# ScalarE in written order during a band attention, with scores, transposes, values and weight requests moved by a slot

## The chip, the cores and the metric

One core of a Trainium2 chip runs the whole program. The metric is device time in microseconds, and lower is better. Before the change three runs took 681.58, 681.89 and 684.72 us; the median is 681.89 us.

## The reference

Three stages follow each other, all in float32. A causal attention with a sliding window and a few sink keys, for 2 batches, 8 heads, 768 positions and 64 dimensions per head; then a mixer with a low-rank token step (rank 32) and a channel step of 512 to 2048 to 512; then a second mixer with a token step of 768 to 256 to 768 and a channel step of 512 to 1536 to 512.

```python
keep = is_sink | in_window                    # key < n_sink, or 0 <= i - j < window
scores = np.where(keep, scale * q @ k.T, -1e9)
a = softmax(scores); x = a @ v
u = x + (x.T @ U @ V).T;  x = u + relu(u @ w_ch1) @ w_ch2
u = x + (relu(x.T @ w_tok1) @ w_tok2).T;  x = u + relu(u @ w_ch1) @ w_ch2
```

## The kernel before

**Attention in slots.** `band_attention` walks 16 units (2 batches, 4 head pairs, 2 halves of the sequence) of three query blocks of 128 each: 48 slots, numbered from 0. In a slot two heads are worked together, over the 224 keys that a block can see. A slot has these steps, by name and line:

- `band_scores` (L191): four matmuls into two PSUM banks, one bank a head (`sc`).
- `band_soft` (L202, L206): for each head VectorE masks and scales into `sm` and takes the minimum `nb`; then ScalarE makes the exponentials `pr` and their sum `den`.
- `band_turn` (L217): TensorE transposes `pr` into `tp`; `band_keep` (L222) copies that to `pt`, on ScalarE for the first block of a unit and on VectorE for the other two.
- `band_values` (L235): the products with the values, into `ot`. `band_out` (L244) copies, `band_back` (L249) transposes back, `band_scale` (L256, L257) divides by the sums on VectorE.

In the kernel before, slot t writes the scores and the softmax of block t, the transposes of block t-2 and the values of block t-4. `load` requests the input of block t+3 (288 KB, `qk`) in slot t; `band_load_values` requests 480 KB a unit. Five input buffers exist. All requests go through SyncE's queue, which stands in written order.

**Work beside the attention.** Between the steps of a slot `weave` lets two side streams advance, each held to a budget per step. One, `lead_stream`, decodes weights: a piece of 512 columns (512 KB of 64-bit words, tile `raw`) is requested with `fetch` (L394), ScalarE takes its absolute value (`clamp`, L402, tile `c`), GpSimd limits it (L403), VectorE rebuilds the float in three steps (L409, L411, L413), and `split` writes a high part on ScalarE (L120) and a low part on GpSimd (L121). There are 15 such pieces during the attention: one of U, two of V, twelve of weights `w`. Three `raw` buffers exist; the first three pieces are requested together at the start and the next with each piece that is done. `FEEDS` says after how many finished units a matrix may be decoded. The other side stream, the fills, is the first mixer's token step (`mix_down`, `mix_up`) and two narrow passes through four of its 16 pairs of weight tiles (`hidden`, `gather`: tiles `hp`, `hh`, `hl`, `accs`).

**What sets the order.** Each engine runs its instructions strictly one after the other. In the attention TensorE and SyncE follow the written order (`manual_schedule` with `MANUAL | ORDERED`). The instructions of ScalarE, VectorE and GpSimd are placed by a planner with its own estimate of when their inputs are there; it may move them ahead of where they are written.

**After the attention** (`layers`, `late_weights`) the same decode and the same channel passes go on with TensorE in written order, and the pieces that are left run through the same `fetch` with three buffers.

Of the kernel before, what the change touches and what calls it, by code (L numbers as in the profile page):

```python
# [10 lines left out]
I32 = mybir.dt.int32  # L11
# [9 lines left out]
P = 128  # L21
# [18 lines left out]
MANUAL = {mybir.EngineType.SP}  # L40
# [1 line left out]
SPREAD = {0: (0.3, 0.3, 0.3, 0.4), 1: (0.7, 0.6, 0.6, 0.7)}  # L42
CHUNK, HOLD = 4, 3
AHEAD = 3
DMA_LAG = 6
WARM = 3
CAP = 1.5
PACE = (9.0, 0.7, 9.0, 9.0)
# [29 lines left out]
class Net:  # L78
# [184 lines left out]
    def band_attention(self, xs):  # L263
        tc = self.tc
        units = [(b, hp, half) for b in range(B) for hp in range(NP) for half in range(2)]
        n = len(units)
        with tc.tile_pool(name="ald", bufs=2) as ld, tc.tile_pool(name="asb", bufs=2) as sb:
            self.sb = sb
            st = [None] * n

            raws = {}

            def load(t):
                if t < 3 * n:
                    raws[t] = self.band_load(t, ld)

            def scale(u):
                self.band_scale(st[u], xs[units[u][0]])
                self.finished = u + 1
                if u + 1 == SWITCH:  # L280
                    self.phase = 1

            def slots():
                for t in range(3 * n + 7):
                    u, ii = divmod(t, 3)
                    if u < n:
                        if ii == 0:
                            st[u] = {"unit": units[u]}
                            self.band_tiles(st[u], sb)
                        self.band_scores(st[u], ii, raws.pop(t))  # L290
                        for e in range(2):
                            self.band_soft(st[u], ii, e, sb)
                        load(t + AHEAD)
                        if ii == 1:
                            self.band_load_values(st[u], ld)
                    yield t
                    u, ii = divmod(t - 2, 3)
                    if 0 <= u < n:
                        self.band_turn(st[u], ii)
                        self.band_keep(st[u], ii)  # L300
                    yield t
                    u, ii = divmod(t - 4, 3)
                    if ii < 2 and 0 <= u < n:
                        for z in ((0, 1), (2,))[ii]:
                            self.band_values(st[u], z)
                        if ii == 1:
                            self.band_out(st[u])
                    if ii == 2 and 0 <= u < n:
                        self.band_back(st[u])
                        scale(u)  # L310
                    yield t

            with tc.manual_schedule(engines=MANUAL | {mybir.EngineType.DVE}):
                self.limits()
                self.band_masks()
                for t in range(AHEAD):
                    load(t)

            with tc.manual_schedule(engines=MANUAL | ORDERED):
                self.weave(slots(), SPREAD)  # L320


# [67 lines left out]


    def fetch(self, src, p0, n):
        raw = self.wp.tile([P, 2 * PIECE], I32, tag="raw", name="raw", bufs=3)[:, :2 * n]
        self.nc.sync.dma_start(raw, src[:, 2 * p0:2 * (p0 + n)])  # L394
        return raw

# [30 lines left out]
    def lead_stream(self):  # L427
        nc, one = self.nc, self.one
        uh, ul = [one.tile([P, NS * RANK], F32R, name=f"u1{z}") for z in "hl"]
        self.vh, self.vl = [one.tile([P, S], F32R, name=f"v{z}") for z in "hl"]  # L430
        pieces = []
        for k, after in enumerate(FEEDS):
            if k > 1:
                self.lead.append(self.weight_tiles(k - 2))
            hi, lo = ((uh, ul), (self.vh, self.vl))[k] if k < 2 else self.lead[k - 2]
            src = self.ins["UV"[k]] if k < 2 else self.ins["w1"][k - 2]
            total = hi.shape[1]
            for p0 in range(0, total, PIECE):
                n = min(PIECE, total - p0)
                pp = slice(p0, p0 + n)  # L440
                pieces.append((after, src, p0, n, hi[:, pp], lo[:, pp], k if p0 + n == total else None))
        raws = {}

        def fetch(k):
            if k < len(pieces):
                raws[k] = self.fetch(*pieces[k][1:4])

        for k in range(3):
            fetch(k)
        yield 0, 0, 0, 0, DMA_LAG  # L450
        yield 0, 0, 0.6, 0.8
        nxt = self.clamp(raws.pop(0))
        for k, (after, _, _, n, hi, lo, done) in enumerate(pieces):
            word, c = nxt
            yield 0, 0, 0, 0, 1
            yield "after", after
            if k + 1 < len(pieces):
                yield 0, 0, 0.6, 0.8
                nxt = self.clamp(raws.pop(k + 1))
            yield from self.assemble(word, c)  # L460
            yield 0, 0, 0, 0, 1
            yield 0, 0, 0.52, 1.23
            self.split(hi, lo, f32(c), nc.scalar.copy, nc.gpsimd)
            yield 0, 0, 0, 0, 2
            fetch(k + 3)
            if done == 0:
                self.u4 = one.tile([P, NS, 4, RANK], F32R, name="u4")
                for c in range(4):
                    src = (ul if c % 2 else uh).rearrange("p (s r) -> p s r", r=RANK)
                    yield 0, 0, 0, 0.3  # L470
                    nc.gpsimd.tensor_copy(self.u4[:, :, c, :], f32(src))
            elif done:
                self.fed = done
# [324 lines left out]
    def whole(self, xs, attention):  # L798
        tc = self.tc
        self.turns, self.phase, self.finished, self.fed = {}, 0, 0, 0  # L800
        with ExitStack() as ctx:
            self.ps = ctx.enter_context(tc.tile_pool(name="ps", bufs=1, space=PSUM))
            self.one = ctx.enter_context(tc.tile_pool(name="one", bufs=1))
            self.two = ctx.enter_context(tc.tile_pool(name="two", bufs=2))
            self.wp = ctx.enter_context(tc.tile_pool(name="wp", bufs=1))
            os_ = [t.rearrange("p s d -> p (s d)").rearrange("p (a c) -> p a c", a=ND) for t in (xs[1], xs[0])]
            self.right = ctx.enter_context(ExitStack())
            x1 = self.right.enter_context(tc.tile_pool(name="x1", bufs=1, side="right"))
            xs = [xs[0], x1.tile([P, NS, DM], F32, name="x1")]
            us = [self.u_tiles(0), None]  # L810
            self.lead, self.sides, self.low = [], [], {}

            def narrow(c):
                cc = slice(c * NARROW, (c + 1) * NARROW)
                return self.channel_pass(us[0], LEAD, cc, os_[0], 6, 1)

            fills = []
            for what in FILLS.split():
                if what[0] == "c":
                    fills.append(((0, 1), narrow, (int(what[1]),)))  # L820
                else:
                    b, d = int(what[1]), int(what[2])
                    if what[0] == "d":
                        fills.append(((0, 1), self.mix_down, (b, d, xs[b], self.nc.gpsimd)))
                    else:
                        fills.append(((0, 1), self.mix_up, (b, d, xs[b], os_[b], us[b], self.nc.gpsimd)))
            self.add_side([((0, 0), self.lead_stream, ())])
            self.add_side(fills)
            attention(xs)
            self.drain(last=1)  # L830
            left = self.sides.pop()
            self.phase = 2
            self.late = ctx.enter_context(tc.tile_pool(name="late", bufs=1, reuse_waits="tile"))
            self.ahead = {g: self.weight_tiles(g) for g in range(len(self.lead), RING)}
            us[1] = self.u_tiles(1)
            with tc.manual_schedule(engines=ORDERED):
                self.ring = dict(enumerate(self.lead))
                self.uses = {g: B if g < LEAD else 2 * B for g in self.ring}
                self.fed = len(self.lead)
                self.add_side([((0, 0), self.late_weights, ())])  # L840
                self.mixed, self.tok = {}, None
                late = [((0, 0), self.mix_up, (1, d, xs[1], os_[1], us[1], self.nc.vector)) for d in range(ND)]
                late.insert(1, ((0, 0), self.mix_down, (1, ND - 1, xs[1], self.nc.vector)))
                self.add_side(late)
                self.weave(self.rest(left, self.layers(us, os_)), PACE)
# [82 lines left out]
```

## Time and profile before

| | us |
|---|---|
| median of three runs | 681.89 |
| the profiled execution | 679.99 |
| its span, first to last instruction | 678.1 |
| TensorE busy in the span | 642.8 |
| VectorE busy | 374.0 |
| ScalarE busy | 226.4 |
| GpSimd busy | 185.8 |

TensorE is busy 95% of the span and has a mean granted clock of 0.97 of full speed. Busy time is an average over two stages: the attention, which ends near 193 us, and the channel passes behind it. A busy TensorE at half clock gets half the work done, so both its idle time and its clock are to be read, stretch by stretch.

### The profile page before, as it was taken

How to read it: one execution, taken by the hardware profiler on the slowest of the kernel's cores; microseconds unless marked ns; L12 is line 12 of the kernel's file. 1: busy time of each engine (PE TensorE's matmuls, PEld its weight loads, DVE VectorE, ACT ScalarE, POOL GpSimd, SP SyncE). 2: the span in 40 equal slices, each digit the busy share in tenths (PEclk: the TensorE clock that was granted, in tenths of full speed). 3: DMA queues.
4: the chain of work that ended last, by engine and by line, in shares of the span. 5: the costliest groups of instructions: out<-in, count | busy, mean ns of one | idle time of the engine just before them, and what ended most of it. 6: DMA issues, size and time to landing. Idle time of an engine off the chain costs nothing.

```text
span 678.1 us, 11317 instructions
## 1 busy us (share of the span) xinstructions
PE 642.8 (95%) x4454; PEld 602.2 (89%) x4454; DVE 374.0 (55%) x792; ACT 226.4 (33%) x552; POOL 185.8 (27%) x208
## 2 busy tenths in 40 slices
PE   7699888889999999999999999999999999999996
PEld 3467657777899999999999999999999999999996
DVE  5676667747355147988882344786241377422223
ACT  4465555435222123433331133533231233211110
POOL 4342424303011025444440022762040244200000
PEclk8889699899999999999999999999999999999999
DMA  7936566455000003343330010313000032000112
GB/s 235 276 118 194 166 215 191 141 175 188 1 1 1 1 17 131 114 129 133 128 128 32 1 63 1 124 67 121 1 1 0 1 125 94 2 0 1 48 47 98
DMA packets 30047, 59.49 MB, mean 88 GB/s; under 512 B 2720, under 2 KB 15648, under 8 KB 29984
## 3 DMA queue, kind: packets, MB, share of 16 engines
q1 hardware_dynamic: 29984, 58.67, 26.8%
q8 instruction: 37, 0.61, 0.4%
q14 instruction: 26, 0.21, 0.1%
HBM read 55.51 MB, written 3.15 MB: 86 GB/s over the span
## 4 chain that ended last, share of the span: by engine, by line
PE 83%; DMA 6%; DVE 5%; ACT 2%; issue 1%; SPq 1%; POOL 1%; ACTq 0%; DVEq 0%; POOLq 0%
PE hp L126 33%; PE accs L652 33%; DMA raw<-in_w 6%; PE ot L235 3%; PE gp L126 3%; PE sc L191 2%; PE tp L217 2%; PE up L126 2%; PE tp L126 2%; DVE c L413 1%; DVE c L411 1%; PE xtp L559 1%; PE xtp L126 1%; ACT pr L206 1%; PE xp L586 1%
## 5 line engine op out<-in xcount | busy, mean ns | idle before, releaser
L126 PE MATMUL hp<-uh,wh 128*128 128x384 f32 (+1 forms) x464 | 155.6, 335 | 5.8 <-DVE hl L633 5.8
L633 DVE SCALAR_TENSOR_TENSOR hl<-hp,hh 128x384 fp32r<-128x384 f32 (+1 forms) x116 | 62.8, 541 | 177.5 <-ACT hh L632 176.7
L652 PE MATMUL accs<-hh,wh 128*128 128x384 f32 (+1 forms) x464 | 154.1, 335 | 0.0
L126 PE MATMUL hp<-uh,wl 128*128 128x384 f32 (+1 forms) x464 | 153.5, 331 | 0.0
L126 PE MATMUL hp<-ul,wh 128*128 128x384 f32 (+1 forms) x464 | 153.4, 331 | 0.0
L652 PE MATMUL accs<-hh,wl 128*128 128x384 f32 (+1 forms) x464 | 152.0, 330 | 0.0
L632 ACT ACTIVATE hh<-hp 128x384 fp32r<-128x384 f32 (+1 forms) x116 | 55.7, 480 | 260.7 <-PE hp L126 260.5
L121 POOL TENSOR_TENSOR wl<-c,wh 128x512 fp32r<-128x512 f32 x56 | 76.2, 1363 | 182.5 <-ACT wh L120 180.3
L652 PE MATMUL accs<-hl,wh 128*128 128x384 f32 (+1 forms) x464 | 97.0, 329 | 0.0
L126 PEld LDWEIGHTS hp<-uh,wh 128*128 128x128 f32 x464 | 87.7, 189 | 9.2 <-DVE hl L633 6.9
L652 PEld LDWEIGHTS accs<-hh,wh 128*128 128x128 f32 x464 | 87.7, 189 | 2.5 <-issue 2.0
L126 PEld LDWEIGHTS hp<-ul,wh 128*128 128x128 f32 x464 | 87.8, 189 | 0.0
L126 PEld LDWEIGHTS hp<-uh,wl 128*128 128x128 f32 x464 | 87.7, 189 | 0.0
L652 PEld LDWEIGHTS accs<-hh,wl 128*128 128x128 f32 x464 | 87.7, 189 | 0.0
L652 PEld LDWEIGHTS accs<-hl,wh 128*128 128x128 f32 x464 | 80.3, 188 | 0.0
L403 POOL TENSOR_SCALAR c<-c 128x512 f32<-128x512 f32 (+2 forms) x65 | 46.1, 709 | 99.2 <-ACT c L402 96.9
L660 DVE TENSOR_TENSOR x<-accs,x 128x384 f32<-128x384 f32 (+1 forms) x118 | 58.7, 556 | 15.1 <-PE accs L652 15.0
L402 ACT ACTIVATE c<-raw 128x512 f32<-128x512 f32 (+2 forms) x65 | 43.0, 662 | 52.8 <-DMA raw<-in_w 27.1
L411 DVE SCALAR_TENSOR_TENSOR c<-raw,c 128x512 int32<-128x512 int32 (+2 forms) x65 | 57.4, 883 | 1.9
L206 ACT ACTIVATE pr<-sm,nb 128x224 f32<-128x224 f32 x96 | 45.4, 474 | 26.9 <-DVE nb L202 26.9
L413 DVE SCALAR_TENSOR_TENSOR c<-raw,c 128x512 int32<-128x512 int32 (+2 forms) x65 | 53.6, 824 | 1.4
L409 DVE TENSOR_SCALAR c<-c 128x512 int32<-128x512 int32 (+2 forms) x65 | 42.3, 651 | 16.9 <-POOL c L403 16.8
(144 smaller groups left out, 713.5 us busy)
## 6 DMA issues: line engine op xcount, KB each, us to landing
raw<-in_w SPq DMA_DIRECT2D x56, 512.0 KB, 3.7
qk<-in_qk SPq DMA_DIRECT2D x47, 288.0 KB, 4.1
vy<-in_vy SPq DMA_DIRECT2D x16, 288.0 KB, 4.3
vx<-in_vx SPq DMA_DIRECT2D x16, 192.0 KB, 3.5
raw<-in_t SPq DMA_DIRECT2D x6, 512.0 KB, 3.5
out<-x SPq DMA_DIRECT2D x16, 192.0 KB, 2.0
raw<-in_V SPq DMA_DIRECT2D x1, 512.0 KB, 5.6
x<-in_qk SPq DMA_DIRECT2D x1, 288.0 KB, 3.3
```

The costliest lines, as they stand in the source:

```text
L121: sub.tensor_tensor(lo, src, f32(hi), ALU.subtract)
L126: self.nc.tensor.matmul(out, lhsT=w, rhs=x, start=start and i == 0, stop=stop and i == n - 1, **kw)
L206: nc.scalar.activation(st["pr", ii][:, e], sm, AF.Exp, bias=nb[:, ii, e:e + 1], scale=-1.0, accum_out=den[:, ii, e:e + 1],)
L402: nc.scalar.activation(f32(c), f32(word[:, :, 1]), AF.Abs)
L403: nc.gpsimd.tensor_scalar(f32(c), f32(c), LARGE, SMALL, ALU.min, ALU.max)
L409: nc.vector.tensor_scalar(c, c, 5, 2, ALU.logical_shift_left, ALU.logical_shift_right)
L411: nc.vector.scalar_tensor_tensor(c, word[:, :, 1], -0x40000000, c, ALU.bitwise_and, ALU.bitwise_or)
L413: nc.vector.scalar_tensor_tensor(c, word[:, :, 0], 29, c, ALU.logical_shift_right, ALU.bitwise_or)
L632: nc.scalar.activation(hh, hp, AF.Relu)
L633: nc.vector.scalar_tensor_tensor(hl, hp, 0.0, f32(hh), ALU.max, ALU.subtract)
L652: self.nc.tensor.matmul(part, lhsT=lhs, rhs=rhs, start=fresh, stop=last and late == 1, skip_group_check=True)
L660: nc.vector.tensor_tensor(oc, a[:, :per * n].rearrange("p (a c) -> p a c", a=per), oc, ALU.add)
```

## The change

ScalarE joins the engines that follow the written order in the attention. In slot t the scores of block t+1 are now written first (with its loads), then the softmax of block t, the transposes of block t-1 and the values of block t-3. In `lead_stream` the first pieces are requested one by one, three steps of the side stream apart, and there are four `raw` buffers, in a pool of their own that is given back after the attention; later pieces take their three buffers from the pool `late`. The lines below the change are numbered 7 to 9 higher afterwards (L394 is L401, L402 is L409, L413 is L420, L527 is L534, L569 is L576, L632 is L639).

```diff
-DMA_LAG = 6
+DMA_LAG = 3
...
+            def ahead(t):
+                u, ii = divmod(t, 3)
+                if u < n:
+                    if ii == 0:
+                        st[u] = {"unit": units[u]}
+                        self.band_tiles(st[u], sb)
+                    self.band_scores(st[u], ii, raws.pop(t))
+                    load(t + AHEAD)
+                    if ii == 1:
+                        self.band_load_values(st[u], ld)
+
             def slots():
-                for t in range(3 * n + 7):
+                ahead(0)
+                for t in range(3 * n + 6):
+                    ahead(t + 1)
                     u, ii = divmod(t, 3)
                     if u < n:
-                        if ii == 0:
...
-                        self.band_scores(st[u], ii, raws.pop(t))
                         for e in range(2):
                             self.band_soft(st[u], ii, e, sb)
-                        load(t + AHEAD)
...
-                    u, ii = divmod(t - 2, 3)
+                    u, ii = divmod(t - 1, 3)
...
-                    u, ii = divmod(t - 4, 3)
+                    u, ii = divmod(t - 3, 3)
...
-            with tc.manual_schedule(engines=MANUAL | ORDERED):
+            with tc.manual_schedule(engines=MANUAL | ORDERED | {mybir.EngineType.Activation}):
...
     def fetch(self, src, p0, n):
-        raw = self.wp.tile([P, 2 * PIECE], I32, tag="raw", name="raw", bufs=3)[:, :2 * n]
+        pool, bufs = (self.raws, self.lead_raws) if self.phase < 2 else (self.late, 3)
+        raw = pool.tile([P, 2 * PIECE], I32, tag="raw", name="raw", bufs=bufs)[:, :2 * n]
...
-        for k in range(3):
-            fetch(k)
-        yield 0, 0, 0, 0, DMA_LAG
+        for k in range(self.lead_raws):
+            fetch(k + 1)
+            yield 0, 0, 0, 0, DMA_LAG
...
-            fetch(k + 3)
+            fetch(k + 1 + self.lead_raws)
...
+            self.lead_raws = 4 if attention == self.band_attention else 3
+            with tc.tile_pool(name="raws", bufs=1) as self.raws:
+                attention(xs)
+                self.drain(last=1)
```

**ScalarE, around slots 7 and 8, before.** A row `pr,den<-sm` is one exponential and two make a slot; `c<-raw` is a clamp, which waits for its weight piece to land; `wh<-c` is the high part that follows the decode.

```order
L402 ACTIVATE c_941<-raw_484 128x512
L527 CAST xh_543<-x0_61 128x384
L206 ACTIVATE pr_449,den_408<-sm_450,nb_407 128x224
L206 ACTIVATE pr_449,den_408<-sm_453,nb_407 128x224
L402 ACTIVATE c_1016<-raw_541 128x512
L120 CAST wh_238<-c_941 128x512
L206 ACTIVATE pr_492,den_408<-sm_493,nb_407 128x224
L206 ACTIVATE pr_492,den_408<-sm_496,nb_407 128x224
L222 COPY pt_507<-tp_508 128x512
```

The same place with the change (the exponentials of slots 8 to 10):

```order
L206 ACTIVATE pr_524,den_399<-sm_525,nb_398 128x224
L206 ACTIVATE pr_524,den_399<-sm_528,nb_398 128x224
L409 ACTIVATE c_531<-raw_335 128x512
L120 CAST vh_251<-c_461 128x256
L206 ACTIVATE pr_564,den_515<-sm_565,nb_514 128x224
L206 ACTIVATE pr_564,den_515<-sm_568,nb_514 128x224
L534 CAST xh_580<-x0_61 128x384
L534 CAST xh_597<-x0_61 128x384
L206 ACTIVATE pr_608,den_515<-sm_609,nb_514 128x224
L206 ACTIVATE pr_608,den_515<-sm_612,nb_514 128x224
L222 COPY pt_615<-tp_616 128x512
```

The clamps of the second and third weight piece (raw_484 and raw_541 before, raw_421 and raw_512 now) have left this place; they stand behind the exponentials of slots 17 and 19. The clamp that is still here (raw_335) is that of the first weight piece, requested five slots before.

**SyncE's queue, around the last weight piece of the attention, before.** `raw` is a weight piece, `qk` the input of a block, `vx` and `vy` the values of a unit; raw_2053 is the last piece of the attention and raw_3056 to raw_3117 belong to the stage behind it.

```order
L179 DMA vy_2015<-in_vy 96x3x256
L394 DMA raw_2053<-in_w1 128x1024
L394 DMA raw_3056<-in_w1 128x1024
L394 DMA raw_3066<-in_w1 128x1024
L170 DMA qk_2078<-in_qk 128x576
L170 DMA qk_2136<-in_qk 128x576
L394 DMA raw_3107<-in_w1 128x1024
L170 DMA qk_2199<-in_qk 128x576
```

With the change:

```order
L179 DMA vy_2191<-in_vy 96x3x256
L170 DMA qk_2241<-in_qk 128x576
L178 DMA vx_2365<-in_vx 128x3x128
L179 DMA vy_2366<-in_vy 96x3x256
L401 DMA raw_3060<-in_w1 128x1024
L401 DMA raw_3070<-in_w1 128x1024
```

The pieces of the later stage now stand behind the attention's last requests. Counted in the two orders for all 15 pieces, by slot: before, the requests stand in slots 0, 0, 0, 3, 7, 9, 20, 21, 28, 30, 31, 33, 34, 36 and 40 and the clamps behind the exponentials of slots 0, 1, 2, 4, 6, 7, 19, 20, 28, 28, 30, 31, 33, 35 and 39. With the change the requests stand in slots 0, 1, 2, 3, 5, 7, 9, 19, 20, 27, 29, 30, 32, 33 and 35 and the clamps behind the exponentials of slots 4, 4, 6, 8, 17, 19, 26, 28, 29, 31, 32, 34, 38, 40 and 41. TensorE's own row of scores, transposes and values is the same as before, with a few side matmuls a slot later.

## Rows read from the trace of the kernel before

**Rows 1.** The page's first line.
```profile
span 678.1 us, 11317 instructions
```

**Rows 2.** Stretches: busy time (count) of PE, PEld, DVE, ACT, POOL; granted clock; DMA.
```profile
12.00:20.50 8.50, 7.59 (x59) 4.86 (x60) 6.85 (x23) 6.07 (x19) 6.46 (x11) 0.60 1.09 311
28.00:31.00 3.00, 0.15 (x6) 0.01 (x2) 0.35 (x1) 1.75 (x5) 1.00 (x2) 0.91 1.05 387
31.00:40.50 9.50, 5.72 (x29) 3.56 (x30) 8.60 (x23) 5.48 (x18) 4.49 (x6) 0.50 0.29 69
40.50:68.00 27.50, 26.70 (x334) 19.85 (x333) 18.11 (x65) 15.37 (x52) 8.17 (x11) 1.00 0.62 182
68.00:71.50 3.50, 0.68 (x7) 0.34 (x8) 0.74 (x3) 2.06 (x6) 0.75 (x2) 0.99 1.07 347
71.50:81.50 10.00, 9.56 (x65) 7.83 (x67) 6.87 (x19) 5.91 (x18) 3.94 (x5) 0.50 0.36 99
95.00:97.00 2.00, 0.20 (x2) 0.00 (x0) 0.00 (x0) 1.01 (x3) 0.32 (x1) 1.00 0.95 329
97.00:102.00 5.00, 4.45 (x32) 3.04 (x32) 4.64 (x13) 3.34 (x10) 2.03 (x4) 0.67 0.40 119
...
104.00:106.00 2.00, 0.21 (x1) 0.21 (x2) 1.70 (x2) 1.00 (x3) 1.00 (x2) 1.00 0.34 134
121.50:125.50 4.00, 1.61 (x22) 1.01 (x21) 3.96 (x8) 1.85 (x8) 1.97 (x2) 1.00 0.81 252
125.50:130.00 4.50, 4.50 (x27) 4.50 (x27) 2.55 (x10) 2.72 (x9) 2.09 (x3) 0.62 0.24 73
146.00:149.00 3.00, 0.81 (x7) 0.57 (x7) 0.63 (x2) 1.27 (x3) 0.61 (x1) 1.00 0.88 348
149.00:154.00 5.00, 5.00 (x46) 4.19 (x47) 4.90 (x11) 2.26 (x7) 2.11 (x2) 0.66 0.26 87
...
300.00:400.00 100.00, 100.00 (x589) 99.83 (x588) 62.02 (x96) 28.93 (x57) 30.12 (x31) 1.00 0.23 79
```

**Rows 3.** Waits in 0 to 200 us, ACT: total us, times, longest.
```profile
ACT c L402 <- DMA raw<-in_w: 27.1, 12, 4.7
```

**Rows 4.** Timeline of ACT, the clamps: start, us, [idle before <-releaser].
```profile
29.25 0.66 ACT L402 ACTIVATE c<-raw 128x512 f32<-128x512 f32 x1 [4.37 <-DMA raw<-in_w]
...
69.22 0.66 ACT L402 ACTIVATE c<-raw 128x512 f32<-128x512 f32 x1 [4.69 <-DMA raw<-in_w]
...
95.94 0.66 ACT L402 ACTIVATE c<-raw 128x512 f32<-128x512 f32 x1 [3.77 <-DMA raw<-in_w]
...
119.73 0.68 ACT L402 ACTIVATE c<-raw 128x512 f32<-128x512 f32 x1 [2.57 <-DMA raw<-in_w]
...
147.40 0.66 ACT L402 ACTIVATE c<-raw 128x512 f32<-128x512 f32 x1 [4.13 <-DMA raw<-in_w]
```

**Rows 5.** The tile raw: durations min/median/max of one decode step, and landing times.
```profile
L413 DVE SCALAR_TENSOR_TENSOR c<-raw,c x65: 357/692/1712, 12.0 to 580.2; 128x512 int32<-128x512 int32 x63, 128x192 int32<-128x192 int32 x1, 128x256 int32<-128x256 int32 x1
...
DMA to landing us min/median/max: 2.8/3.7/8.5
```

**Rows 6.** Scores (L191) alone in one stretch; eight matmul records make a slot.
```profile
40.50:68.00 27.50, 7.39 (x90) 2.57 (x90) 1.00 0.62 182
```

**Rows 7.** Groups of 0 to 200 us, by form: the exponential and the read of its sum.
```profile
L206 ACT ACTIVATE pr<-sm,nb 128x224 f32<-128x224 f32 x96 | 45.4, 474 | 26.9 <-DVE nb L202 26.9
...
L206 ACT ACTIVATION_READ_ACCUMULATOR pr<-sm,nb 128x1 f32 x96 | 18.0, 187 | 0.0
```

**Rows 8.** Timeline of 103 to 106 us: POOL, DVE and PE.
```profile
103.40 1.45 POOL L570 TENSOR_TENSOR ul<-x,uh 128x384 fp32r<-128x384 f32 x1
...
104.03 1.37 DVE L413 SCALAR_TENSOR_TENSOR c<-raw,c 128x512 int32<-128x512 int32 x1
...
105.79 0.39 PE L126 MATMUL hp<-uh,wh 128*128 128x256 f32 x1 [2.13 <-DVE hl L633]
```

**Rows 9.** Timeline of ACT behind the attention: the first high parts of later weights.
```profile
246.22 1.14 ACT L120 CAST wh<-c 128x512 fp32r<-128x512 f32 x2 [1.59 <-PE accs L652]
```

More of the change, by code (lines that the diff above doesn't have):

```diff
@@ L281, in scale @@
                     self.phase = 1
+            def ahead(t):
[8 more added lines that the diff above has]
+                        self.band_load_values(st[u], ld)
             def slots():
-                for t in range(3 * n + 7):
+                ahead(0)
+                for t in range(3 * n + 6):
+                    ahead(t + 1)
                     u, ii = divmod(t, 3)
                     if u < n:
-                        if ii == 0:
-                            st[u] = {"unit": units[u]}
-                            self.band_tiles(st[u], sb)
-                        self.band_scores(st[u], ii, raws.pop(t))
                         for e in range(2):
                             self.band_soft(st[u], ii, e, sb)
-                        load(t + AHEAD)
-                        if ii == 1:
-                            self.band_load_values(st[u], ld)
                     yield t
-                    u, ii = divmod(t - 2, 3)
+                    u, ii = divmod(t - 1, 3)
                     if 0 <= u < n:
@@ L442, in lead_stream, with fetch @@
         raws = {}
-        def fetch(k):
-            if k < len(pieces):
-                raws[k] = self.fetch(*pieces[k][1:4])
-        for k in range(3):
-            fetch(k)
-        yield 0, 0, 0, 0, DMA_LAG
+        def fetch(end):
+            for z in range(len(raws), min(end, len(pieces))):
+                raws[z] = self.fetch(*pieces[z][1:4])
+        for k in range(self.lead_raws):
+            fetch(k + 1)
+            yield 0, 0, 0, 0, DMA_LAG
         yield 0, 0, 0.6, 0.8
-        nxt = self.clamp(raws.pop(0))
+        nxt = self.clamp(raws[0])
         for k, (after, _, _, n, hi, lo, done) in enumerate(pieces):
@@ L458, in lead_stream @@
                 yield 0, 0, 0.6, 0.8
-                nxt = self.clamp(raws.pop(k + 1))
+                nxt = self.clamp(raws[k + 1])
             yield from self.assemble(word, c)
@@ L828, in whole @@
             self.add_side(fills)
-            attention(xs)
-            self.drain(last=1)
+            self.lead_raws = 4 if attention == self.band_attention else 3
+            with tc.tile_pool(name="raws", bufs=1) as self.raws:
+                attention(xs)
+                self.drain(last=1)
             left = self.sides.pop()
```

## The prediction

> **What bounds the kernel now.** I read the first line of the page for the span, 678.1 us [rows 1], and then the stretches. Behind the attention TensorE has nothing to give: in 300 to 400 us it is busy 100.00 of 100 us at full clock [rows 2]. So only the attention, the first 193 us, can become shorter, and there the reader is to look at two columns of the stretches, TensorE's busy time and its granted clock. From 40.5 to 68 us it is busy 26.70 of 27.50 us at clock 1.00, while 11 slots go by (90 matmul records, eight a slot) [rows 2, 6]: 2.4 us a slot, nothing wrong. Around that stand stretches with gaps, and behind most gaps a stretch at clock 0.50, the lower of the two levels. The list of waits names one item first for ScalarE: 27.1 us, in 12 waits, before L402 until a weight piece has landed [rows 3]. The timeline shows five of them next to the gaps, at 29.25, 69.22, 95.94, 119.73 and 147.40 us, 2.57 to 4.69 us each [rows 4]. ScalarE runs in order, so the exponentials behind such a clamp wait too; then the transposes wait, then TensorE.
>
> The cause is in the order: a clamp stands from two slots ahead of the slot of its own request to two slots behind it, and a request takes 2.8 to 8.5 us to land [rows 5]. The planner believed the pieces were there.
>
> **What the five stalls cost.** The cost of each is TensorE's idle time plus half of its busy time at half clock; the share at half clock is twice what is missing from 1.00. All from [rows 2]:
> - near 30 us: idle (3.00 - 0.15) + (9.50 - 5.72) = 6.6, and 5.72 / 2 = 2.9 for the clock: 9.5 us;
> - near 70 us: idle 2.82 + 0.44 = 3.26, and 9.56 / 2 = 4.78: 8.0 us;
> - near 96 us: idle 1.80 + 0.55 = 2.35, clock 0.66 x 4.45 / 2 = 1.5: 3.8 us;
> - near 123 us: idle 4.00 - 1.61 = 2.4, clock 0.76 x 4.50 / 2 = 1.7: 4.1 us;
> - near 147 us: idle 3.00 - 0.81 = 2.2, clock 0.68 x 5.00 / 2 = 1.7: 3.9 us.
>
> Together 29.3 us.
>
> **The change, part by part.**
>
> *ScalarE in written order.* No instruction is added or removed; the 15 clamps move to 3 to 17 slots behind their requests. At 2.4 us a slot the shortest distance is 7.2 us and the usual one 9.6 us or more, against a landing of 3.7 us in the median and 8.5 at most [rows 5]. So the waits go and I book the whole 29.3. The bounds: 0 if the pieces land later still; 29.3 and not more for these five.
>
> What is late next? In written order ScalarE also waits for TensorE and VectorE (the copies `pt`, `hh`, `tt`, `uh`), with exponentials queued behind, and behind those the transposes. An exponential pair takes 2 x (0.474 + 0.187) = 1.3 us [rows 7] and its transposes come a slot of TensorE work later, 2.4 us. That leaves 1.1 us a slot for such a wait, so I book it at nothing; without that cover it is the rival that ends slower.
>
> *Scores a slot ahead, transposes and values a slot sooner.* TensorE's row stays as it was, since both parts moved by one slot against the softmax. What moves is the softmax against the side work on ScalarE and VectorE, and the requests `qk`, which keep their distance to their scores. Booked at nothing; the cover is TensorE's full row, as between 40.5 and 68 us.
>
> *First pieces one by one, four buffers.* The blocks' inputs now pass the first weight requests on SyncE's queue, and a fourth weight piece comes before slot 10. Up to the scores of slot 14 there land 15 inputs of 288 KB, five sets of values of 480 KB and 3008 KB of weights, 9728 KB in all, 10.0 million bytes. At the 311 GB/s that 12 to 20.5 us moved [rows 2] that is 32 us, as long as 14 slots of 2.4 us take TensorE. So the first 36 us become tight on transfers. I book 2.0 us lost, between 0 and 5. That same stretch, 12 to 20.5 us, loses 0.9 idle + 0.80 x 7.59 / 2 = 3.0 to the clock, 3.9 us, today, partly behind early clamps; because of the tight transfers I take 0 of it back, with 3.9 as the bound.
>
> *Later pieces out of the attention's queue.* Two pieces of the next stage that were requested in the attention now come behind its last request. Their first use, the high part at 246.22 us, waits for TensorE to give up the old weights [rows 9], not for the transfer. Cover: the 53 us from the attention's end to there; cost 0.
>
> *VectorE's own order* is still the planner's. Near 105 us TensorE was idle for 1.8 us of 2 [rows 2] because `hl` came behind two decode steps on VectorE. One of them took 1.37 us, 0.692 being the median [rows 5], and lay beside a GpSimd subtraction from 103.40 to 104.85 [rows 8]. That stays: 0 gained. I book one more such case, 1.8 us, among the decodes that now meet other work. Bounds: a gain of 1.8, and a loss in the rival below.
>
> The Trainium skill, SBUF — State Buffer, section "SBUF: two separate sides", says that VectorE and GpSimd share a port pair as an exclusive lock, also for a VectorE instruction with two SBUF inputs, so that the later one is blocked until the other is done. By that rule L413 would have ended at 104.85 + 0.69 = 105.54; the trace has 105.40, and agrees. By the rule this stall stays, as I have it; without it I would add 1.8 us to the gain.
>
> **Sum.** 29.3 - 2.0 - 1.8 = 25.5 us. The profiled execution took 679.99 us, so it becomes 654.5; the median of the runs stands 1.9 above that execution, 681.9, and becomes **656.4 us**. Most that the terms allow: 29.3 + 3.9 + 1.8 = 35.0, which gives 646.9, and about 2 more for small gaps.
>
> **The rivals.**
> 1. *VectorE and GpSimd take over.* With the weights in time, the decodes of slots 28 to 41, eight pieces, collide as near 105 us, 1.8 us each. For it: VectorE was busy 1.70 of 2 us there and 3.96 of 4 us at 121.5 to 125.5 [rows 2]. Against it: it was only 18.1 of 27.5 us busy in the good stretch, and its decodes come as densely after slot 28 as before. Gain 29.3 - 2.0 - 14.4 = 12.9: 669 us. The port rule named above is the mechanism; the price is the row's.
> 2. *Transfers bound the start.* The first stall stays as a wait for `qk`, 9.5 us: gain 25.5 - 9.5 = 16.0, 666 us. For it: the transfer engines were full (1.05 to 1.09) at 12 to 31 us. Against it: 0.29 in the 9.5 us behind, so there was room.
> 3. *Slower: ScalarE's written order.* An instruction that waits for TensorE (say `hh` on a product just issued) holds the next exponentials, and their transposes hold TensorE. If that costs 0.75 us in each of 48 slots, 36 us go, 10.5 more than the sum: 692 us. It decides from 25.5 / 48 = 0.53 us a slot. For it: the planner had moved instructions past such waits. Against it: the 1.1 us of room.
> 4. *It does not do what it says:* clamps still meet late pieces, since transfers slow with a shorter attention. Gain under 3 us, 680 us. Against it: 7.2 us of distance, and an average transfer load of 0.62 in the good stretch.
>
> **Chances.** My forecast has 0.68, the first rival 0.12, the second 0.11, the third 0.05, the fourth 0.04. A measurement of this kernel tells 0.5%, 3.4 us, from no change. Forecast and rivals 1 and 2 are faster: 0.91; rival 4 the same: 0.04; rival 3 slower: 0.05. The range goes from 645, all bounds on the good side with the small gaps, to 671, which takes in the first two rivals.
>
> **What would show it.** In the profile of the changed kernel ScalarE's waits for `raw` before the clamp fall from 27.1 us to under 4; TensorE's first 165 us have clock 1.00 from about 35 us on, with no gap over 2 us but one or two before `hp`; the attention's last transposes come some 25 us sooner; behind it nothing changes. Wrong would be: gaps before the scores until `nb` although no clamp waits (rival 1), before scores until `qk` (rival 2), or before transposes until `pr` in every slot (rival 3).

## The result and the profile after

The changed kernel took 654.3 us, the median of 4 runs (654.21 to 655.07); the kernel before took 683.3 us beside it. The ratio is 0.958 (95% interval 0.955 to 0.961): faster by 4.2%, and 2.1 us below the predicted 656.4. Its profiled execution took 654.38 us; the page's first lines:

```profile
span 652.6 us, 11317 instructions
...
PE 632.4 (97%) x4454; PEld 594.1 (91%) x4454; DVE 375.2 (57%) x792; ACT 224.6 (34%) x552; POOL 188.5 (29%) x208
...
PEclk9999999989999999999999999999999999999999
```

The span is 25.5 us shorter [rows 1]. TensorE does the same 4454 operations with 10.4 us less busy time (642.8 before). I put that down to the clock, since the mean granted clock rose from 0.970 to 0.996. The other 15.1 us are idle time: 678.1 - 642.8 = 35.3 before, 20.2 now. One slice of the clock's line is below 9. By the medians the gain is larger than by these two spans, 683.3 - 654.3 = 29.0 us: the profiled execution of the kernel before, 679.99 us, was quicker than its four runs (681.58 to 685.01).

Stretches of the changed kernel, the columns as in [rows 2]:

```profile
10.00:40.00 30.00, 26.29 (x308) 18.00 (x308) 24.11 (x81) 19.46 (x65) 11.59 (x19) 1.00 1.07 313
...
70.00:100.00 30.00, 27.04 (x297) 21.21 (x298) 25.21 (x69) 19.20 (x60) 14.98 (x16) 1.00 0.66 203
...
130.00:160.00 30.00, 27.74 (x275) 23.47 (x274) 17.86 (x51) 13.77 (x44) 10.98 (x13) 0.94 0.19 62
```

The first of them in the kernel before:

```profile
10.00:40.00 30.00, 20.38 (x184) 12.78 (x178) 22.02 (x65) 17.61 (x54) 13.60 (x20) 0.73 0.81 244
```

Before, this stretch lost 9.6 us idle and 0.27 x 20.38 = 5.5 us to the clock; now it loses 3.7 and nothing, with the transfer engines full throughout (1.07).

Waits of the changed kernel in 0 to 200 us (total us, times, longest):

```profile
ACT hh L639 <- PE hp L126: 42.4, 17, 6.1
ACT pr L206 <- DVE nb L202: 13.5, 12, 5.4
...
PE sc L191 <- DVE nb L202: 3.8, 7, 0.8
PE hp L126 <- DVE hl L640: 2.3, 3, 0.9
```

The clamp's wait for `raw`, 27.1 us [rows 3], is in the list no more. ScalarE waits longest for `hp`, but TensorE waits only 2.3 us for `hl`, which follows. In the kernel before the two last rows read:

```profile
PE sc L191 <- DVE nb L202: 13.8, 7, 5.5
PE hp L126 <- DVE hl L633: 5.8, 4, 2.2
```

The last transposes of the attention, after and before:

```profile
161.96 0.60 PE L217 MATMUL tp<-ident,pr 128*128 128x128 f32 x4
```
```profile
187.05 0.60 PE L217 MATMUL tp<-ident,pr 128*128 128x128 f32 x4
```

They come 25.1 us sooner; behind them 490.0 and 490.4 us follow. So 25.1 of the 25.5 us lie in the attention.

### The profile page after: what moved, and what is told of

Same layout as the page of the kernel before. It is cut to its first block, busy times and chain, and to the rows that moved or that the text cites. A ratio compares the mean times of both kernels' runs of the same rounds, so it can differ in the third digit from the quotient of the medians.

```text
span 652.6 us, 11317 instructions
## 1 busy us (share of the span) xinstructions
PE 632.4 (97%) x4454; PEld 594.1 (91%) x4454; DVE 375.2 (57%) x792; ACT 224.6 (34%) x552; POOL 188.5 (29%) x208
## 4 chain that ended last, share of the span: by engine, by line
PE 90%; DVE 5%; issue 2%; ACT 2%; POOL 1%; DVEq 0%; ACTq 0%; POOLq 0%
PE hp L126 35%; PE accs L659 35%; PE sc L191 3%; PE ot L235 3%; PE tp L217 3%; PE gp L126 3%; PE up L126 2%; PE tp L126 2%; PE xtp L126 1%; PE xtp L566 1%; DVE sm L202 1%; PE xp L593 1%; PE w L112 1%; DVE c L418 1%; DVE x L667 1%
## 5 line engine op out<-in xcount | busy, mean ns | idle before, releaser
L639 ACT ACTIVATE hh<-hp 128x384 fp32r<-128x384 f32 (+1 forms) x116 | 55.7, 481 | 277.8 <-PE hp L126 277.7
L418 DVE SCALAR_TENSOR_TENSOR c<-raw,c 128x512 int32<-128x512 int32 (+2 forms) x65 | 59.5, 915 | 1.6
L420 DVE SCALAR_TENSOR_TENSOR c<-raw,c 128x512 int32<-128x512 int32 (+2 forms) x65 | 53.4, 821 | 1.4
L409 ACT ACTIVATE c<-raw 128x512 f32<-128x512 f32 (+2 forms) x65 | 43.0, 663 | 24.9 <-POOL wl L121 24.8
L206 ACT ACTIVATE pr<-sm,nb 128x224 f32<-128x224 f32 x96 | 45.3, 474 | 13.5 <-DVE nb L202 13.5
```

Source lines behind the costliest of these rows:

```text
L206: nc.scalar.activation(st["pr", ii][:, e], sm, AF.Exp, bias=nb[:, ii, e:e + 1], scale=-1.0, accum_out=den[:, ii, e:e + 1],)
L409: nc.scalar.activation(f32(c), f32(word[:, :, 1]), AF.Abs)
L418: nc.vector.scalar_tensor_tensor(c, word[:, :, 1], -0x40000000, c, ALU.bitwise_and, ALU.bitwise_or)
L420: nc.vector.scalar_tensor_tensor(c, word[:, :, 0], 29, c, ALU.logical_shift_right, ALU.bitwise_or)
L639: nc.scalar.activation(hh, hp, AF.Relu)
```

## The experiments

Three things were changed at once: ScalarE's order, the slots and the weight requests. The prediction gave all of the gain to ScalarE's order. The theories: **A**, as predicted, a clamp must stand behind its piece and ScalarE's order does that; **B**, the softmax needs the shift by a slot, since in written order ScalarE waits for its own slot's scores with side work queued behind; **C**, the weights must be requested earlier. Each ratio is to runs of the kernel before on the same chip.

**1. ScalarE in written order, nothing else** (against the kernel before).

```diff
-            with tc.manual_schedule(engines=MANUAL | ORDERED):
+            with tc.manual_schedule(engines=MANUAL | ORDERED | {mybir.EngineType.Activation}):
```


> Only ScalarE is put into written order; slots and weight requests as before. Theory A (a clamp must stand well behind its request): the clamps now stand 2 to 11 slots behind their requests instead of -2 to 2, so the waits for raw before the clamp fall from 27.1 us to under 8 (the pieces with a distance of 2 slots still wait a little), and the time is 655 to 664 us, at least three quarters of the gain. Theory B (the gain comes from the softmax having a slot more room): little of it is here, 672 to 682 us. Theory C (the weights have to be requested earlier, with four buffers): the waits stay over 15 us, 670 to 680 us.

Measured: 670.6 us, ratio 0.983 (0.978 to 0.988), 11.5 us gained. Its waits:

```profile
ACT pr L206 <- DVE nb L202: 56.0, 37, 6.1
...
PE hp L126 <- DVE hl L633: 4.9, 3, 2.6
```

No clamp waits for `raw`, and still less than half of the gain is there: A's mechanism holds, A's size falls.

**2. The slots and the requests, ScalarE left to the planner** (against the changed kernel).

```diff
-            with tc.manual_schedule(engines=MANUAL | ORDERED | {mybir.EngineType.Activation}):
+            with tc.manual_schedule(engines=MANUAL | ORDERED):
```


> The slots and the weight requests of the change, but ScalarE's order again by the planner. Theory A: the planner moves the clamps back to -1 to 1 slots from their requests, the waits for raw stay at 15 to 27 us, and the time is 674 to 684 us. Theory B: 656 to 668 us. Theory C: 658 to 668 us, waits for raw under 10 us.

Measured: 675.5 us, ratio 0.991 (0.988 to 0.994). The clamps wait again, with U and V 21.6 us in all, which is A's outcome:

```profile
ACT c L409 <- DMA raw<-in_w: 17.6, 7, 4.1
```

**3. The changed kernel with the slots of before.** The scores are again those of block t, the transposes those of t-2, the values those of t-4.

```diff
-                ahead(0)
-                for t in range(3 * n + 6):
-                    ahead(t + 1)
+                for t in range(3 * n + 7):
...
+                        self.band_scores(st[u], ii, raws.pop(t))
...
-                    u, ii = divmod(t - 1, 3)
+                    u, ii = divmod(t - 2, 3)
...
-                    u, ii = divmod(t - 3, 3)
+                    u, ii = divmod(t - 4, 3)
```


> ScalarE in written order and the weight requests of the change; scores, softmax, transposes and values in the slots of before. Theory A: the distances of the clamps are the same 3 to 18 slots, no wait for raw, 653 to 659 us. Theory B: in written order ScalarE now waits for the scores of its own slot with the side work behind it, TensorE's waits for hl and for the exponentials grow by 8 us or more, 663 us or more.

Measured: 666.5 us, ratio 0.978 (0.973 to 0.982): the time is B's. The waits:

```profile
ACT pr L206 <- DVE nb L202: 54.1, 38, 4.8
```

A place where it costs TensorE, on the timeline of 85 to 92 us:

```profile
85.80 1.30 POOL L121 TENSOR_TENSOR wl<-c,wh 128x512 fp32r<-128x512 f32 x1 [0.38 <-ACT wh L120]
85.92 1.73 DVE L412 SCALAR_TENSOR_TENSOR c<-raw,c 128x512 int32<-128x512 int32 x1
...
88.03 1.01 DVE L414 SCALAR_TENSOR_TENSOR c<-raw,c 128x512 int32<-128x512 int32 x1
...
88.97 0.38 DVE L202 CUSTOM_DVE_ANT_0 sm<-sc,m 128x224 f32<-128x224 f32 x1
...
89.39 0.48 ACT L206 ACTIVATE pr<-sm,nb 128x224 f32<-128x224 f32 x1 [3.26 <-DVE nb L202]
...
90.73 0.37 ACT L633 ACTIVATE hh<-hp 128x256 fp32r<-128x256 f32 x1
...
91.14 0.42 DVE L634 SCALAR_TENSOR_TENSOR hl<-hp,hh 128x256 fp32r<-128x256 f32 x1 [1.48 <-ACT hh L633]
...
91.62 0.58 PE L126 MATMUL hp<-uh,wh 128*128 128x256 f32 x1 [2.57 <-DVE hl L634]
```

Two decode steps run before the mask on VectorE, which the planner still orders. The exponential waits 3.26 us for it; `hh`, written behind the exponentials, follows only then, then `hl`, and TensorE has stood for 2.57 us. In the changed kernel the exponentials of that place had found their masks done, and TensorE's gap is a third of that:

```profile
85.02 0.38 ACT L639 ACTIVATE hh<-hp 128x256 fp32r<-128x256 f32 x1 [1.77 <-PE hp L126]
...
85.91 0.39 PE L126 MATMUL hp<-uh,wh 128*128 128x256 f32 x1 [0.93 <-DVE hl L640]
```

So B's mechanism is right in one part and wrong in another. ScalarE does wait, 38 times, but for VectorE's mask (`nb`) of its own slot's scores, and TensorE's matmuls have no wait for `pr` in the list. What comes late is the side work written behind the exponentials: TensorE's waits for `hl`, `xl`, `t` and `ul` are 11.8 us together against 5.1 in the changed kernel, of 8.2 us more idle time in all.

**4. The changed kernel with the requests of before**: three buffers, the first three pieces together, `DMA_LAG` 6.

```diff
-DMA_LAG = 3
+DMA_LAG = 6
...
-        for k in range(self.lead_raws):
-            fetch(k + 1)
-            yield 0, 0, 0, 0, DMA_LAG
+        for k in range(3):
+            fetch(k)
+        yield 0, 0, 0, 0, DMA_LAG
...
-            fetch(k + 1 + self.lead_raws)
+            fetch(k + 3)
```


> ScalarE in written order and the slots of the change; three raw buffers and the three first pieces together, as before. Theory A: distances of 1 to 11 slots; some waits for raw come back (2 to 8 us), 654 to 661 us. Theory C: waits for raw over 15 us, 668 us or more.

Measured: 658.7 us, ratio 0.965 (0.960 to 0.970): A, not C. The clamps wait 2.5 us for U and 0.9 us for V, and never for `w`. The 4.4 us above the changed kernel lie at the start: from 10 to 40 us TensorE is idle for 6.0 us and loses 2.6 to the clock, against 3.7 and nothing. There blocks' inputs are late, three of them requested behind both pieces of V on SyncE's queue (timeline of TensorE, and a stretch):

```profile
17.14 0.56 PE L191 MATMUL sc<-qk 64*64 64x224 f32 x2 [2.21 <-DMA qk<-in_qk]
18.83 1.02 PE L191 MATMUL sc<-qk 64*64 64x224 f32 x6 [1.13 <-DVE nb L202]
```
```profile
20.00:30.00 10.00, 8.93 (x91) 5.98 (x90) 6.90 (x26) 5.88 (x18) 3.23 (x5) 0.72 0.94 310
```

**5. The shift alone**, the slots of the change in the kernel before (the slots' part of the diff and nothing else):

```diff
+                ahead(0)
+                for t in range(3 * n + 6):
+                    ahead(t + 1)
...
-                    u, ii = divmod(t - 2, 3)
+                    u, ii = divmod(t - 1, 3)
...
-                    u, ii = divmod(t - 4, 3)
+                    u, ii = divmod(t - 3, 3)
```


> The kernel before with only the slots of the change; the planner places ScalarE's instructions and the weight requests are as before. If the slot shift brings its 12 us by itself: 668 to 674 us. If it only pays together with ScalarE in written order, because the planner moves exponentials past the waiting work by itself: 678 to 686 us, with the waits before the clamp as in the kernel before, 20 to 30 us.

Measured: 684.6 us, ratio 1.003 (1.000 to 1.006): nothing. ScalarE's waits are those of the kernel before:

```profile
ACT pr L206 <- DVE nb L202: 29.1, 25, 5.1
ACT c L408 <- DMA raw<-in_w: 22.9, 11, 4.7
...
ACT c L408 <- DMA raw<-in_U: 4.3, 1, 4.3
```

So the shift pays with ScalarE's order, 0.983 to 0.965 (runs 1 and 4), and not without it.

**6. The requests one by one, with six buffers, ScalarE left to the planner** (the requests' part of the diff in the kernel before, and):

```diff
+            self.lead_raws = 6 if attention == self.band_attention else 3
```


> The kernel before with weight pieces requested one by one and six raw buffers; the planner still places ScalarE's instructions. Theory A (the waits for raw come from where the planner puts the clamps, not from late requests): ScalarE's waits before the clamp stay at 15 to 30 us, and the time is 673 to 684 us. The theory that the pieces were asked for too late: with six buffers the waits fall under 8 us and the time to 662 us or less.

Measured: 676.2 us, ratio 0.990 (0.984 to 0.996). The waits fell from 28.4 to 14.6 us, with those for U and V, just under the range that A gave, and are not gone:

```profile
ACT c L403 <- DMA raw<-in_w: 11.7, 5, 3.6
...
ACT c L403 <- DMA raw<-in_U: 1.7, 1, 1.7
ACT c L403 <- DMA raw<-in_V: 1.2, 2, 0.8
```

Each clamp has moved up with its request: it runs from two slots ahead of the request's slot to two behind, as before. Six buffers did not buy distance here; that the planner believes the piece is there is my reading of its order, not shown.

**7. Scores two slots ahead, transposes in the softmax's own slot** (against the changed kernel).

```diff
-                for t in range(3 * n + 6):
-                    ahead(t + 1)
+                ahead(1)
+                for t in range(3 * n + 5):
+                    ahead(t + 2)
...
-                    u, ii = divmod(t - 1, 3)
+                    u, ii = divmod(t, 3)
...
-                    u, ii = divmod(t - 3, 3)
+                    u, ii = divmod(t - 2, 3)
```


> The changed kernel with the scores two slots ahead of the softmax and the transposes in the softmax's own slot, values two slots later. Theory B (the softmax needs about a slot of TensorE work on each side of it): the exponentials find their scores done, but the transposes have only the four score matmuls of their own slot ahead of them, some 2.4 us at most, and wait for pr; slower than the changed kernel by 5 to 40 us, 660 to 695 us, with TensorE's waits tp <- pr at the top of the list and ScalarE's waits before L206 below the 13.5 us of the changed kernel. The theory that only the distance of the scores counts: 650 to 656 us.

Measured: 702.9 us, ratio 1.031 (1.025 to 1.037). The loss was expected, though not so large (695 at most), and its place was not: TensorE's first wait is that of the scores, and its matmuls have none for `pr` in the list.

```profile
PE sc L191 <- DVE nb L202: 31.5, 29, 2.3
```

**8. Scores two slots ahead, the rest as in the changed kernel.** There are two PSUM banks for scores, one slot's worth, which suggests what happened in run 7.

```diff
-                for t in range(3 * n + 6):
-                    ahead(t + 1)
+                ahead(1)
+                for t in range(3 * n + 6):
+                    ahead(t + 2)
```


> The changed kernel with the scores two slots ahead and transposes and values where the change has them. The scores have two PSUM banks, one slot's worth, so the scores of block t+2 must wait until the masks of block t+1 are done. If that wait on the banks is what made the run with both moved slow: 685 to 710 us again, with sc <- nb the first wait of TensorE. If that run was slow because its transposes stood too close behind the exponentials: 650 to 660 us, since they have their slot back here.

Measured: 702.0 us, ratio 1.029 (1.023 to 1.035). TensorE waits 29.8 us for `nb` before the scores. Giving the transposes their slot back changes nothing, so it is the wait on the banks; at a place on the timeline the scores begin 0.14 us behind the end of the mask that they wait for:

```profile
64.81 0.39 DVE L202 CUSTOM_DVE_ANT_0 sm<-sc,m 128x224 f32<-128x224 f32 x1
...
65.13 0.09 DVE L202 DVE_READ_ACCUMULATOR2_ANT nb<- 128x1 f32 x1
...
65.36 0.60 PE L191 MATMUL sc<-qk 64*64 64x224 f32 x6 [2.00 <-DVE nb L202]
```

With two banks, one slot ahead is as far as the scores can go here.

**9. Three slots between scores and transposes** (transposes of t-2, values of t-4, scores still ahead).

```diff
-                for t in range(3 * n + 6):
+                for t in range(3 * n + 7):
...
-                    u, ii = divmod(t - 1, 3)
+                    u, ii = divmod(t - 2, 3)
...
-                    u, ii = divmod(t - 3, 3)
+                    u, ii = divmod(t - 4, 3)
```


> The changed kernel with transposes two slots behind the scores' successor, as before the change (transposes of block t-2, values of block t-4), and the scores still a slot ahead: three slots between scores and transposes instead of two. Theory B, if more room behind the exponentials is worth anything: 648 to 653 us. If the room ahead of the exponentials is all that the shift brought: 653 to 658 us, the slot longer at the end included.

Measured: 661.3 us, ratio 0.970 (0.965 to 0.975), worse than either number. More room behind the exponentials buys nothing. TensorE has a slot less to do while the pipeline fills, 14.78 us busy in 10 to 30 us against 17.11, which is 2.3 of the 6.0 us that the span is longer:

```profile
10.00:30.00 20.00, 14.78 (x172) 9.40 (x173) 15.38 (x55) 13.25 (x43) 8.39 (x15) 1.00 1.07 338
```
```profile
10.00:30.00 20.00, 17.11 (x204) 11.32 (x203) 16.64 (x58) 13.86 (x46) 9.48 (x16) 1.00 1.08 329
```

(the second row is the changed kernel's). Another 2.0 us is a wait of TensorE for `wh` at 137.21 us; the rest is not worked out.

**10. The first requests twice as far apart** (against the changed kernel).

```diff
-DMA_LAG = 3
+DMA_LAG = 6
```


> The changed kernel with the first weight pieces requested six steps apart instead of three. If the full transfer engines cost the changed kernel its 3.6 us of idle TensorE between 16 and 32 us: 650 to 653 us, with the gaps there below 1.5 us. If the work beside the attention is what sets the pace behind it, the decodes come later and the time is 654 to 660 us.

Measured: 662.2 us, ratio 0.972 (0.967 to 0.978), slower than both numbers. Idle time in 10 to 40 us is 4.2 us, against 3.7: the full transfer engines are not relieved. The loss is in 80 to 95 us, a gap before the scores and some 4.5 us of clock:

```profile
83.98 1.02 PE L191 MATMUL sc<-qk 64*64 64x224 f32 x6 [1.65 <-DVE nb L202]
```
```profile
80.00:85.00 5.00, 3.35 (x26) 2.26 (x25) 4.61 (x11) 2.51 (x8) 3.06 (x4) 0.86 0.30 78
85.00:90.00 5.00, 4.22 (x31) 3.39 (x33) 4.71 (x12) 2.54 (x9) 2.25 (x3) 0.50 0.99 284
90.00:95.00 5.00, 5.00 (x46) 3.06 (x42) 3.09 (x9) 2.54 (x8) 1.60 (x2) 0.61 0.82 288
```

**11 and 12. VectorE, or GpSimd, in written order as well** (against the changed kernel; run 12 with `Pool` in place of `DVE`).

```diff
-            with tc.manual_schedule(engines=MANUAL | ORDERED | {mybir.EngineType.Activation}):
+            with tc.manual_schedule(engines=MANUAL | ORDERED | {mybir.EngineType.Activation, mybir.EngineType.DVE}):
```


> The changed kernel with VectorE in written order as well. If the decodes that the planner puts ahead of the masks cost what is left (ScalarE's 13.5 us of waits before L206 for nb, TensorE's few gaps of 0.8 to 1.3 us before hp, tp and sc): 648 to 653 us. If VectorE in written order then waits for GpSimd's and ScalarE's parts of the decode with masks queued behind, as ScalarE could have: 658 to 680 us.

> The changed kernel with GpSimd in written order as well. GpSimd is 29% busy and TensorE waits for it some 3 us in the attention (xl, ul); nothing of the softmax runs on it, so both theories say no difference that can be told: 651 to 658 us. Outside that, an operation of GpSimd that waits for a late one of VectorE holds the limits of the next decode, and it is slower.

Measured: VectorE 720.9 us, ratio 1.053 (1.046 to 1.059), far outside both ranges; GpSimd 659.4 us, ratio 0.967 (0.962 to 0.972), slightly above its range. With VectorE in order its waits in 0 to 200 us begin with

```profile
DVE pt L222 <- PE tp L217: 40.8, 23, 3.0
```

and ScalarE's wait before L206 is back at 58.0 us: masks stand behind copies that wait for TensorE, and not, as was expected, behind the decode's wait for other engines. With GpSimd in order the longest new wait of TensorE is 1.9 us, for `wh`.

No version beat the changed kernel. Run 4's interval (from 0.960) touches that of the change (to 0.961); the others lie apart, run 12's (from 0.962) by little.

## Why the prediction was right, and where it was not

The forecast case came: 25.5 us booked, a span 25.5 us shorter, 29.0 us by the medians. That the spans agree to the tenth is luck, twice over: the kernel before varies by more than the 2.1 us between forecast and result, and the sum was right by terms that made up for each other.

**The stalls: right that they could go.** No clamp waits for a weight piece now, and idle time and clock were both to be counted: 12.6 us of the 29.3 were booked as clock and 10.4 us of busy time went. Whether 29.3 us was their price no run shows by itself, since run 1 took the waits away and brought others.

**"I book the whole 29.3" on ScalarE's order, "booked at nothing" for the scores a slot ahead: wrong.** ScalarE's order alone brings 1.7%, 11.5 us (run 1); the shift brings 0.983 - 0.965 = 1.8% on top, 12 us, with the old requests, and 0.978 - 0.958 = 2.0% with the new ones. The cover named for the shift, TensorE's full row, was read in a kernel whose planner may move side work past a late mask. In written order that freedom is gone: ScalarE waits 54 to 56 us for its masks and 13.5 with the shift. Rival 3 had the engine right and the direction wrong: not a side instruction holding the exponentials and their transposes, but exponentials that wait for their masks holding the side instructions (run 3). It costs 12 us / 48 = 0.25 us a slot without the shift; 0.53 would have made the change slower. The 1.1 us of cover was counted behind the exponentials, where run 9 shows that more room buys nothing; what was short was the room between the scores and the exponentials.

**"2.0 us lost" for the requests, 0 of the early 3.9 us taken back: wrong in sign.** The transfers are as tight as foreseen (1.07), but the new requests bring more than that: run 4 loses 4.4 us without them, and runs 5 and 2 (1.003 and 0.991), which differ in the requests alone, show it too. Runs 1 and 3 (0.983 and 0.978) point the same way, but their intervals overlap. The start, 10 to 40 us, gave 15.1 - 3.7 = 11.4 us, where 9.5 - 2.0 = 7.5 were booked.

**The other four stalls: 19.8 - 1.8 = 18.0 us booked, 25.5 - 11.4 = 14.1 came.** Small gaps remain, after the first 8 us none longer than 1.32 us, at 133.72. The term of 1.8 us for one more `hl` case had the wrong sign by itself: those waits fell from 5.8 to 2.3 us.

**VectorE's decode beside GpSimd (rival 1): it came, its price did not.** In run 3 L412 began at 85.92, 0.12 us behind a GpSimd subtraction that ended at 87.10; it took 1.73 us and ended at 87.65, 0.55 us behind that. Undisturbed steps of this width took 0.68 and 0.73 us in that run. The changed kernel has the same:

```profile
81.57 1.46 POOL L121 TENSOR_TENSOR wl<-c,wh 128x512 fp32r<-128x512 f32 x1 [2.04 <-ACT wh L120]
...
82.29 1.28 DVE L418 SCALAR_TENSOR_TENSOR c<-raw,c 128x512 int32<-128x512 int32 x1
```

From 28 us to the attention's end 14 such steps begin inside a GpSimd subtraction, 5 in the kernel before, and every one ends 0.55 us behind the subtraction's end. The rule of the Trainium skill, SBUF — State Buffer, section "SBUF: two separate sides", has the later one blocked until the other is done; the trace agrees, though the end comes sooner than a whole step (0.69 us) behind. Together the 14 steps took 5.0 us longer than undisturbed ones, the 5 before 3.2. But TensorE's waits for `nb` and `hl` fell from 19.6 to 6.1 us, so the 1.8 us a case that rival 1 booked did not come. The scores' lead is not shown to be the reason, since in run 3, without it, TensorE's waits for `nb` were 3.3 us, as short as the 3.8 here.

**Rivals 2 and 4.** TensorE's waits for `qk` are not in the list, and no clamp waits for a weight piece. **Behind the attention** nothing changed, 490.0 against 490.4 us.

Not tried: a version with four PSUM banks for the scores, and the first requests one by one without the fourth buffer, so how the 4.4 us share between these two is open. Why VectorE's masks come behind decodes in run 10 is not settled.

## What to carry to other kernels

Taking an engine from a planner to written order removes the planner's mistakes and its help at once: in the same edit, give the instructions that wait on another engine a stage's distance to what they wait for, and price the two together. Here one alone gave 11.5 us, the other none, and both 23.5 (run 4). Free buffers did not keep a consumer from being placed at its request (run 6); its place in the order did. The distance ends where the buffers of the producer end: one slot of scores ahead fitted the two PSUM banks, two slots cost some 48 us.

## What was not expected of the hardware

A gap shorter than those of the five clamp stalls can be followed by TensorE's lower level (1.2 GHz). In the kernel before the shortest of the five was 2.19 us in one piece:

```profile
148.85 0.39 PE L126 MATMUL hp<-uh,wh 128*128 128x256 f32 x1 [2.19 <-DVE hl L633]
```

In the changed kernel the gap of 1.32 us is:

```profile
133.72 0.30 PE L126 MATMUL tp<-xh,u 128*128 128x128 f32 x1 [1.32 <-DVE x L667]
```
```profile
134.00:136.00 2.00, 2.00 (x20) 1.34 (x18) 1.37 (x4) 0.69 (x3) 1.60 (x2) 0.83 0.00 0
136.00:139.00 3.00, 3.00 (x36) 2.54 (x36) 2.94 (x9) 1.70 (x6) 2.57 (x2) 0.55 0.03 5
139.00:142.00 3.00, 3.00 (x36) 2.43 (x36) 1.71 (x6) 1.86 (x6) 0.68 (x1) 1.00 0.06 18
```

The clock is 0.55 from 136 to 139 us, mostly the lower level, and full behind it: with the stretch before, 1.7 us are lost. In run 10 the gap of 1.65 us at 83.98 us was followed by 0.50 and then 0.61, 4.5 us lost by the rows of run 10, and a gap of 1.28 us there by none:

```profile
97.88 0.38 PE L126 MATMUL hp<-uh,wh 128*128 128x256 f32 x1 [1.28 <-DVE hl L640]
```
```profile
98.00:100.00 2.00, 2.00 (x18) 2.00 (x19) 0.68 (x1) 0.00 (x0) 0.00 (x0) 1.00 0.89 333
```

In the kernel before, the longer gap of 2.13 us at 105.79 us [rows 8] was followed by full clock too:

```profile
106.00:108.00 2.00, 2.00 (x20) 2.00 (x19) 0.75 (x2) 0.33 (x2) 1.72 (x2) 1.00 0.03 8
```

So a short gap may cost nothing, its own length again or more than twice that. Its length alone does not decide it; what does, the rows do not settle.
